# Local queries of a sparse attention spread into a block-diagonal tile of their own by GpSimd copies

## The chip, the cores and the metric

One core of a Trainium2 chip runs the whole program. The metric is the device time of one execution in microseconds (us). Engines are named as the profile names them: PE is TensorE (PEld its weight loads), DVE is VectorE, ACT is ScalarE, POOL is GpSimd, SP is SyncE, whose queue issues most of the DMA transfers.

## What is computed

An attention over 8 batches of 8 heads, 576 positions and 64 channels per head, all in fp32, followed by a mixture of 8 experts with one expert per token:

```
rel = pos[:, None] - pos[None, :]
mask_local = (rel >= 0) & (rel < 32)                      # heads 0 to 3
mask_strided = (rel >= 0) & (pos[None, :] % 32 == pos[:, None] % 32)   # heads 4 to 7
scores = where(mask, q @ k.T / 8, -1e9); attn = softmax(scores) @ v
x = attn as [4608 tokens, 512]; expert = argmax(x @ w_gate)
out[token] = gate[token] * (relu(x[token] @ w1[expert]) @ w2[expert])
```

Only the local heads are concerned here: each block of 32 queries needs the 64 keys of its own block and the one before it.

## The kernel before, in words

The attention is cut into 40 tasks, five for each batch (`tasks`, line 762). Tasks 0 and 1 of a batch (k = 0 and 1) each hold 16 query blocks of one pair of local heads; tasks 2 to 4 hold the rest of the local blocks and the strided heads. So task numbers 0, 1, 5, 6, 10, 11 and so on to 36 are the 16 local ones. Each task goes through four stages:

- `stage_s` (line 388): a matmul against the identity writes the mask into a PSUM bank (line 391), then small matmuls add the scores. In a local task they are 16 calls of `wide` (line 396), one for each query block: the stationary operand (the weights, 128 partitions by 64 columns) is block diagonal, the 32 queries of head h in partitions 64h to 64h+63 and zeros elsewhere, and the moving operand is the block's 64 keys of both heads. An fp32 matmul is two instruction pairs of load and matmul in the records, so a local task shows 32 of each on line 399, 512 in all.
- `softmax` (line 337): DVE takes maxima (`nm`, line 340) and subtracts, ACT takes the exponential, DVE sums and inverts (`ri`, line 349), POOL multiplies (line 350).
- `stage_t` (line 438), three tasks later (`LAG_T`): PE transposes the probabilities (line 441), ACT copies them out of PSUM.
- `av_local` and `av_strided`, four tasks later (`LAG_AV`): PE multiplies by the values (line 466 for the local heads, line 455 for the others).

The order of PE's instructions is that of the loop on line 790, by hand: in iteration i the transposes of task i-3, then the scores of task i, then the values of the batch that is complete. The order on the other engines is worked out by a scheduler, and each engine takes its own queue strictly in that order. After the scores of task i the loop calls `load_qk(i + 5)` (line 364), the queries and keys of the same k in the next batch, and `load_v`. Between the tasks of a batch PE also makes the routing to experts and, from the fourth batch on, the first expert tokens (`fillers`, line 632); their weight chunks of 1 MB come by `wload` (line 202) and are split into a high and a low part by `wsplit` (line 209: ACT casts on line 212, DVE subtracts on line 213). After the attention come the experts, on which the change has no hand.

The two local tasks of a batch have a tile each, `qkl[k]` (line 355), used again in every batch: 512 columns for head 0's queries, 512 for head 1's, 544 for the keys. The halves that must be zero are cleared once. `load_qk` fills the rest by three transfers of 64 partitions each. Queries lie there with the block number as the fast index, so that `wide` takes each 16th column:

```
q = qkl[k][:, 0:2 * LQ].rearrange("p (q j) -> p q j", j=LB)
k0 = 2 * LQ + QB * j
nc.tensor.matmul(sb[64 * i:64 * i + 64, col:col + 64], q[:, :, j], qkl[k][:, k0:k0 + 64],
                 start=False, stop=last, tile_position=(0, 64 * i))
```

With LB = 16 and 4 bytes an element, neighbouring columns of these weights are 64 bytes apart in a partition. The weights on line 466 (`vt[:, 64 * h:64 * h + 64]`) have the same shape and array position and lie in adjacent columns.

Of the kernel before, what the change touches and what calls it, by code (L numbers as in the profile page):

```python
# [7 lines left out]
F32 = mybir.dt.float32  # L8
# [9 lines left out]
B, S, D = 8, 576, 64  # L18
# [4 lines left out]
QB = 32  # L23
# [19 lines left out]
LAG_AV = 4  # L43
EXP = (0, 2, 4, 6)
# [92 lines left out]
def moe_attn(ctx, tc, qk, vv, wg, wcat, blob0, blob, out):  # L137
# [170 lines left out]
    with ExitStack() as actx:  # L308
        inp = actx.enter_context(tc.tile_pool(name="inp", bufs=NBK - 2))
# [45 lines left out]
        qkl = [loc.tile([128, 2 * LQ + LK], F32, name=f"qkl{k}") for k in range(2)]  # L355
        pTl = [loc.tile([128, 2, 512], F32, name=f"pTl{k}") for k in range(2)]
        for k in range(2):
            nc.vector.memset(qkl[k][64:128, 0:LQ], 0.0)
            nc.gpsimd.memset(qkl[k][0:64, LQ:2 * LQ], 0.0)
# [4 lines left out]
        def load_qk(i):  # L364
            if i < len(tasks):
                b, k = tasks[i]
                if k < 2:
                    o = QKO[k]
                    nc.sync.dma_start(out=qkl[k][64:128, LQ:], in_=qk[b, 64:128, o:o + LQ + LK])
                    nc.sync.dma_start(out=qkl[k][0:64, 0:LQ], in_=qk[b, 0:64, o:o + LQ])  # L370
                    nc.sync.dma_start(out=qkl[k][0:64, 2 * LQ:], in_=qk[b, 0:64, o + LQ:o + LQ + LK])
                    return
                t = inp.tile([128, max(QKW[2:])], F32, name="qk")
                loaded[b, "qk", k] = t
                nc.sync.dma_start(out=t[:, 0:QKW[k]], in_=qk[b, :, QKO[k]:QKO[k + 1]])

        def load_v(i):
            if i < len(tasks):
                b, k = tasks[i]
                t = inv.tile([128, VVW[0]], F32, name="vl", bufs=2) if k < 2 else inv.tile([128, max(VVW[2:])], F32, name="vt", bufs=3)  # L380
# [7 lines left out]
        def stage_s(b, k):  # L388
# [7 lines left out]
            def wide(j, i, col, last):  # L396
                q = qkl[k][:, 0:2 * LQ].rearrange("p (q j) -> p q j", j=LB)
                k0 = 2 * LQ + QB * j
                nc.tensor.matmul(sb[64 * i:64 * i + 64, col:col + 64], q[:, :, j], qkl[k][:, k0:k0 + 64],  # L399
# [254 lines left out]
        def slot_tables():  # L654
            rem = rt.tile([128, E], F32, name="rem")
            nc.vector.tensor_scalar(out=rem, in0=cnt, scalar1=-float(BASE), scalar2=0.0, op0=ALU.add, op1=ALU.max)
            it128 = rt.tile([128, 32], F32, name="it128")
# [118 lines left out]
        load_qk(0)  # L776
        nc.vector.tensor_copy(out=identb, in_=ident)
        make_masks()
        load_qk(1)
        load_qk(2)  # L780
# [8 lines left out]
        with tc.manual_schedule(engines={mybir.EngineType.PE}):  # L789
            for i in range(nt + LAG_AV):  # L790
# [14 lines left out]
                if i < nt:  # L805
                    filling()
                    pvs[i] = stage_s(*tasks[i])
                    load_qk(i + NBK)
# [170 lines left out]
def host_layout(q, k, v, moe_w_gate, moe_w1, moe_w2):  # L979
# [31 lines left out]
    for k in range(NBK):  # L1011
        for key, o in QK[k][0].items():
            o += QKO[k]
            if key == "l":
                parts = [lq[:, k, :, 0:LQ], lk[:, k, :, 0:LK]]
                parts[0] = parts[0].reshape(B, 128, LB, QB).transpose(0, 1, 3, 2).reshape(B, 128, LQ)
# [54 lines left out]
```

## Time and profile before

| what | us |
|---|---|
| median of 3 runs (lowest, highest) | 695.56 (695.17, 698.36) |
| the profiled execution, whole | 701.65 |
| its span, first to last instruction | 699.8 |
| outside the span (701.65 - 699.8) | 1.85 |
| PE busy in the span | 656.6 (94%) |
| DVE busy | 432.8 (62%) |
| ACT busy | 354.1 (51%) |
| POOL busy | 150.1 (21%) |

The profiled execution is one execution and was 6.09 us longer than the median of the runs. Its mean granted TensorE clock was 0.972. A busy PE is not PE at its peak: matmuls are pipelined and their ends are modelled, so the times from start to start in the timeline say more on its pace than the length of one. The attention takes roughly the first 215 us of the span; the first 95 us or so are attention alone.

### The profile page before, as it was taken

To read this page: it belongs to the slowest core of one execution; us is meant where nothing else is said; L and a number is where in the kernel's file an instruction comes from. 1 tells how busy PE (TensorE), PEld (TensorE's weight loads), DVE (VectorE), ACT (ScalarE), POOL (GpSimd) and SP (SyncE) were. 2 spreads that over 40 slices of the span, in tenths; PEclk is the share of its full clock that TensorE was granted. 3 is DMA by queue.
4 is the path that set the end of the run, shared out by engine and by line. 5 is a ranking of instruction groups with operands and counts; after the bars stand their busy time and mean duration, and the time that the engine had idled before them with its cause. 6 is when DMAs were issued, how large, how long until landed. Compare 5 with 4: busy or idle time off the path is not lost.

```text
span 699.8 us, 14771 instructions
## 1 busy us (share of the span) xinstructions
PE 656.6 (94%) x5996; PEld 548.9 (78%) x5996; DVE 432.8 (62%) x796; ACT 354.1 (51%) x617; POOL 150.1 (21%) x168
## 2 busy tenths in 40 slices
PE   5899799699989899999999999998999999999997
PEld 3777578587778778888888888887988878988885
DVE  5756768747476369888425867336675357583464
ACT  1556466455445455366225656336564246572363
POOL 3223222520311031127004132013132032010021
PEclk9999799999959999999999999999999999999999
DMA  9888989884842765558525968336766347765140
GB/s 284 257 239 251 303 255 294 287 290 141 286 129 92 287 215 174 193 208 304 234 112 166 352 215 286 117 133 234 296 245 223 120 138 270 267 225 180 61 180 21
DMA packets 36695, 149.85 MB, mean 214 GB/s; under 512 B 5261, under 2 KB 5645, under 8 KB 26384
## 3 DMA queue, kind: packets, MB, share of 16 engines
q1 hardware_dynamic: 24576, 118.50, 50.3%
q0 software_dynamic: 6432, 20.26, 8.1%
q10 hardware_dynamic: 5616, 10.12, 4.0%
q8 instruction: 48, 0.79, 0.5%
q14 instruction: 23, 0.19, 0.1%
HBM read 129.69 MB, written 20.22 MB: 214 GB/s over the span
## 4 chain that ended last, share of the span: by engine, by line
PE 72%; issue 13%; DVE 6%; ACT 4%; POOL 1%; another core or an unknown queue 1%; DMA 1%; POOLq 1%; SPq 0%; ACTq 0%
PE t L287 8%; PE t L288 7%; PE t L289 7%; PE y L276 6%; PE y L278 6%; PE y L277 6%; PE s L399 4%; PE t L441 2%; PE s L412 2%; PE v L265 2%; PE s L276 2%; PE s L278 2%; PE s L277 2%; PE v L455 1%; PE s L898 1%
## 5 line engine op out<-in xcount | busy, mean ns | idle before, releaser
L213 DVE TENSOR_TENSOR wlo<-raw,whi 128x1024 fp32r<-128x1024 f32 x160 | 192.6, 1221 | 88.4 <-ACT whi L212 76.6
L212 ACT CAST whi<-raw 128x1024 fp32r<-128x1024 f32 x160 | 163.3, 1050 | 67.5 <-PE s L278 26.1
L287 PE MATMUL t<-xh,whi 128*128 128x256 f32 (+1 forms) x384 | 126.1, 330 | 3.2 <-ACT xh L221 1.3
L288 PE MATMUL t<-xl,whi 128*128 128x256 f32 (+1 forms) x384 | 124.5, 325 | 0.3 <-DVE xl L222 0.3
L289 PE MATMUL t<-xh,wlo 128*128 128x256 f32 (+1 forms) x384 | 124.2, 324 | 0.0
L292 ACT ACTIVATE hh<-t 128x256 fp32r<-128x256 f32 (+1 forms) x96 | 43.5, 453 | 118.9 <-PE t L289 113.3
L293 DVE SCALAR_TENSOR_TENSOR hl<-t,hh 128x256 fp32r<-128x256 f32 (+1 forms) x96 | 48.9, 509 | 77.1 <-ACT hh L292 76.9
L287 PEld LDWEIGHTS t<-xh,whi 128*128 128x128 f32 x384 | 73.0, 191 | 11.7 <-ACT xh L221 2.1
L288 PEld LDWEIGHTS t<-xl,whi 128*128 128x128 f32 x384 | 73.4, 191 | 7.5 <-DVE xl L222 1.1
L289 PEld LDWEIGHTS t<-xh,wlo 128*128 128x128 f32 x384 | 73.2, 191 | 6.4 <-DVE wlo L213 0.8
L276 PE MATMUL y<-whi,hh 128*128 128x512 f32 x192 | 76.4, 398 | 0.0
L277 PE MATMUL y<-wlo,hh 128*128 128x512 f32 x192 | 75.1, 391 | 0.0
L278 PE MATMUL y<-whi,hl 128*128 128x512 f32 x192 | 75.0, 396 | 0.0
L350 POOL TENSOR_TENSOR prob<-prob,ri 128x512 f32<-128x512 f32 x40 | 43.4, 1084 | 147.2 <-DVE ri L349 91.8
L248 POOL DMA_INDIRECT out_dram<-y,oids x24 | 26.9, 1119 | 215.6 <-DVE y L247 166.6
L340 DVE TENSOR_REDUCE nm<-s 128x8 f32<-128x512 f32 x40 | 27.4, 686 | 29.7 <-PE s L399 19.5
L155 ACT COPY xT<-v 128x270 f32<-128x270 f32 (+1 forms) x80 | 30.2, 476 | 30.1 <-PE v L466 11.8
L278 PEld LDWEIGHTS y<-whi,hl 128*128 128x128 f32 x192 | 35.8, 188 | 8.4
L276 PEld LDWEIGHTS y<-whi,hh 128*128 128x128 f32 x192 | 36.2, 188 | 6.6 <-issue 0.8
L277 PEld LDWEIGHTS y<-wlo,hh 128*128 128x128 f32 x192 | 36.3, 189 | 5.7
L344 ACT ACTIVATE prob<-prob 128x512 f32<-128x512 f32 x40 | 25.3, 632 | 26.1 <-DVE prob L343 25.2
L399 PEld LDWEIGHTS s<-qkl 128*64 128x64 f32 x512 | 30.8, 209 | 8.1 <-issue 7.8
(173 smaller groups left out, 1170.9 us busy)
## 6 DMA issues: line engine op xcount, KB each, us to landing
raw<-in_wcat_dram SPq DMA_DIRECT2D x80, 1024.0 KB, 5.6
xd<-xr ACTq DMA_DIRECT2D x36, 264.0 KB, 5.5
vl<-in_vv_dram SPq DMA_DIRECT2D x16, 512.0 KB, 6.3
qkl<-in_qk_dram SPq DMA_DIRECT2D x16, 264.0 KB, 4.0
vt<-in_vv_dram SPq DMA_DIRECT2D x16, 256.0 KB, 5.6
qk<-in_qk_dram SPq DMA_DIRECT2D x8, 484.0 KB, 6.0
qk<-in_qk_dram SPq DMA_DIRECT2D x8, 432.0 KB
qk<-in_qk_dram SPq DMA_DIRECT2D x8, 396.0 KB, 5.7
```

The costliest lines, as they stand in the source:

```text
L212: nc.scalar.copy(out=hi[:, sl], in_=raw[:, sl])
L213: i = nc.vector.tensor_tensor(out=lo[:, sl], in0=raw[:, sl], in1=hi[:, sl].bitcast(F32), op=ALU.subtract)
L276: nc.tensor.matmul(yb[t], hh[:, ts], whi[:, w], start=(j == 0), stop=False)
L277: nc.tensor.matmul(yb[t], hh[:, ts], wlo[:, w], start=False, stop=False)
L278: nc.tensor.matmul(yb[t], hl[:, ts], whi[:, w], start=False, stop=(j == 7))
L287: nc.tensor.matmul(hb[:, 0:n], whi[:, w], xh[:, dc, :], start=(dc == 0), stop=False)
L288: nc.tensor.matmul(hb[:, 0:n], whi[:, w], xl[:, dc, :], start=False, stop=False)
L289: nc.tensor.matmul(hb[:, 0:n], wlo[:, w], xh[:, dc, :], start=False, stop=(dc == 3))
L292: nc.scalar.activation(out=hh[:, 0:n], in_=hb[:, 0:n], func=AF.Relu)
L293: nc.vector.scalar_tensor_tensor(out=hl[:, 0:n], in0=hb[:, 0:n], scalar=0.0, in1=hh[:, 0:n].bitcast(F32), op0=ALU.max, op1=ALU.subtract)
L350: lastp[0] = nc.gpsimd.tensor_tensor(out=pv, in0=pv, in1=ri.unsqueeze(2).broadcast_to([128, 8, 64]), op=ALU.mult)
L399: nc.tensor.matmul(sb[64 * i:64 * i + 64, col:col + 64], q[:, :, j], qkl[k][:, k0:k0 + 64], start=False, stop=last, tile_position=(0, 64 * i))
```

## The change

The queries get a tile of their own, `qbd[k]`, 16 blocks of 64 adjacent columns, zeroed once by DVE. `qkl[k]` holds 512 columns of queries and 544 of keys, as they come, for both heads one above the other, and is filled by one transfer of 128 partitions. `spread(i)` copies each head's queries from it to their place on the diagonal with two POOL copies of 64 partitions by 16 by 32 elements; it is called two tasks ahead (`AHEAD`). The loaded tiles of tasks 2 to 4 get a name and a buffer each instead of three buffers under one name, and one small table is put into a buffer that is in use anyway.

```diff
-        inp = actx.enter_context(tc.tile_pool(name="inp", bufs=NBK - 2))
+        inp = actx.enter_context(tc.tile_pool(name="inp", bufs=1))
...
-        qkl = [loc.tile([128, 2 * LQ + LK], F32, name=f"qkl{k}") for k in range(2)]
+        qkl = [loc.tile([128, LQ + LK], F32, name=f"qkl{k}") for k in range(2)]
+        qbd = [loc.tile([128, LB, 2 * QB], F32, name=f"qbd{k}") for k in range(2)]
...
-            nc.vector.memset(qkl[k][64:128, 0:LQ], 0.0)
-            nc.gpsimd.memset(qkl[k][0:64, LQ:2 * LQ], 0.0)
+            nc.vector.memset(qbd[k].rearrange("p j q -> p (j q)"), 0.0)
...
-                    o = QKO[k]
-                    nc.sync.dma_start(out=qkl[k][64:128, LQ:], in_=qk[b, 64:128, o:o + LQ + LK])
-                    nc.sync.dma_start(out=qkl[k][0:64, 0:LQ], in_=qk[b, 0:64, o:o + LQ])
-                    nc.sync.dma_start(out=qkl[k][0:64, 2 * LQ:], in_=qk[b, 0:64, o + LQ:o + LQ + LK])
+                    nc.sync.dma_start(out=qkl[k], in_=qk[b, :, QKO[k]:QKO[k + 1]])
                     return
-                t = inp.tile([128, max(QKW[2:])], F32, name="qk")
+                t = inp.tile([128, QKW[k]], F32, name=f"qk{k}")
...
+        def spread(i):
+            if i < len(tasks) and tasks[i][1] < 2:
+                k = tasks[i][1]
+                for h in range(2):
+                    hs = slice(64 * h, 64 * h + 64)
+                    nc.gpsimd.tensor_copy(out=qbd[k][hs, :, QB * h:QB * h + QB],
+                                          in_=qkl[k][hs, 0:LQ].rearrange("p (j q) -> p j q", q=QB))
...
-                q = qkl[k][:, 0:2 * LQ].rearrange("p (q j) -> p q j", j=LB)
-                k0 = 2 * LQ + QB * j
-                nc.tensor.matmul(sb[64 * i:64 * i + 64, col:col + 64], q[:, :, j], qkl[k][:, k0:k0 + 64],
+                k0 = LQ + QB * j
+                nc.tensor.matmul(sb[64 * i:64 * i + 64, col:col + 64], qbd[k][:, j, :], qkl[k][:, k0:k0 + 64],
                                  start=False, stop=last, tile_position=(0, 64 * i))
...
-            it128 = rt.tile([128, 32], F32, name="it128")
+            it128 = scratch(32)
...
                     pvs[i] = stage_s(*tasks[i])
+                    spread(i + AHEAD)
                     load_qk(i + NBK)
```

PE's own order is the same. On POOL the copies stand between the multiplications of the softmax, one of which belongs to each task (`prob` is a task's probabilities; the numbers behind the names are those of the buffers in the program). The multiplications of tasks 5 to 8 and the first rows of tokens (`xr`) in POOL's queue before:

```order
L350 TENSOR_TENSOR prob_389<-prob_389,ri_394 128x512
L350 TENSOR_TENSOR prob_466<-prob_466,ri_471 128x512
L350 TENSOR_TENSOR prob_511<-prob_511,ri_516 128x512
L350 TENSOR_TENSOR prob_585<-prob_585,ri_590 128x512
L505 COPY xr_688<-gt_328 128x16
```

and the same place now, from task 4's multiplication to that of task 8 (`qbd0` and `qkl0` belong to k = 0, here task 10, `qbd1` and `qkl1` to k = 1, here task 11):

```order
L351 TENSOR_TENSOR prob_347<-prob_347,ri_352 128x512
L380 COPY qbd0_135<-qkl0_133 64x16x32 x2
L351 TENSOR_TENSOR prob_389<-prob_389,ri_394 128x512
L351 TENSOR_TENSOR prob_464<-prob_464,ri_469 128x512
L380 COPY qbd1_136<-qkl1_134 64x16x32 x2
L351 TENSOR_TENSOR prob_507<-prob_507,ri_512 128x512
L351 TENSOR_TENSOR prob_581<-prob_581,ri_586 128x512
```

So the copies for task 10 stand ahead of the multiplication of task 5, and those for task 11 ahead of task 7's. A batch later the copies for tasks 15 and 16 stand between the multiplications of tasks 10 and 11:

```order
L351 TENSOR_TENSOR prob_673<-prob_673,ri_678 128x512
L351 TENSOR_TENSOR prob_742<-prob_742,ri_747 128x512
L380 COPY qbd0_135<-qkl0_133 64x16x32 x2
L380 COPY qbd1_136<-qkl1_134 64x16x32 x2
L351 TENSOR_TENSOR prob_817<-prob_817,ri_822 128x512
```

In the batches behind, the copies for task 20 stand ahead of task 15's multiplication, those for 21 ahead of 16's, those for 25 and 26 ahead of 21's, those for 30 ahead of 25's and those for 31 ahead of 26's.

On SP the weight chunks (`raw`) moved forward as well. Before, the first one was issued in the middle of the loads of the fifth batch (`vt` and `vl` are values):

```order
L375 DMA qk<-in_qk_dram 128x968
L382 DMA vt<-in_vv_dram 128x640
L375 DMA qk<-in_qk_dram 128x792
L382 DMA vt<-in_vv_dram 128x512 x2
L375 DMA qk<-in_qk_dram 128x864
L204 DMA raw<-in_wcat_dram 128x2048
L369 DMA qkl_133<-in_qk_dram 64x1056
L370 DMA qkl_133<-in_qk_dram 64x512
```

and now two stand among the loads of the third batch:

```order
L369 DMA qkl_134<-in_qk_dram 128x1056
L373 DMA qk_516<-in_qk_dram 128x968
L388 DMA vt_552<-in_vv_dram 128x640
L373 DMA qk_592<-in_qk_dram 128x792
L388 DMA vt_686<-in_vv_dram 128x512
L388 DMA vt_624<-in_vv_dram 128x512
L205 DMA raw<-in_wcat_dram 128x2048
L373 DMA qk_684<-in_qk_dram 128x864
L205 DMA raw<-in_wcat_dram 128x2048
L369 DMA qkl_133<-in_qk_dram 128x1056
```

With them their two pairs of casts on ACT and subtractions on DVE moved to the tasks around number 10.

## Rows read from the trace of the kernel before

**Rows 1.** The page: the span, and busy time, share of the span and instructions of each engine.

```profile
span 699.8 us, 14771 instructions
PE 656.6 (94%) x5996; PEld 548.9 (78%) x5996; DVE 432.8 (62%) x796; ACT 354.1 (51%) x617; POOL 150.1 (21%) x168
```

**Rows 2.** The chain of work that ended last, over the whole span: shares of the span by engine, tile written and line.

```profile
by line: issue 12.9%; PE t L287 7.6%; PE t L288 7.5%; PE t L289 7.5%; PE y L276 5.9%; PE y L278 5.9%; PE y L277 5.7%; PE s L399 4.0%; PE t L441 2.2%; PE s L412 1.8%; PE v L265 1.7%; PE s L276 1.6%; PE s L278 1.6%; PE s L277 1.6%; PE v L455 
```

**Rows 3.** Groups of instructions by line and shape over the whole span: line, engine, operation, tiles, weights as partitions*columns, out<-in, count | busy us, mean ns of one | idle us before them and what ended it.

```profile
L399 PE MATMUL s<-qkl 128*64 128x64 f32 x512 | 33.1, 289 | 2.0 <-DMA qkl<-in_qk_dram 2.0
L399 PEld LDWEIGHTS s<-qkl 128*64 128x64 f32 x512 | 30.8, 209 | 8.1 <-issue 7.8 <-DMA vl<-in_vv_dram 0.3
...
L412 PEld LDWEIGHTS s<-qk 64*54 64x54 f32 x640 | 21.2, 141 | 6.2 <-issue 3.6 <-DMA vt<-in_vv_dram 0.8 <-DMA qk<-in_qk_dram 0.5
...
L466 PE MATMUL v<-pTl,vl 128*64 128x64 f32 x512 | 17.3, 223 | 1.1 <-issue 1.0
...
L466 PEld LDWEIGHTS v<-pTl,vl 128*64 128x64 f32 x512 | 16.1, 138 | 1.7 <-issue 1.6
```

**Rows 4.** The same chain between 20 and 62 us: the shares of this stretch by line, then three of its pieces in order of time (start us, us, what).

```profile
by line: PE s L399 19.2%; ACT xT L155 11.4%; PE t L441 10.6%; PE v L455 9.3%; PE v L466 8.9%; PE s L412 7.7%; PE y L516 5.9%; ACT prob L344 4.7%; PE s L391 4.6%; PE y L508 4.6%; issue 3.7%; PE y L523 3.6%; POOL prob L350 2.5%; PE s L407 1.7
...
42.45 2.00 PE s L399 x32
44.45 1.87 PE v L466 x64
...
59.52 0.94 PE s L412 x32
```

**Rows 5.** Busy time of each engine in stretches of 20 us: stretch, its length, busy us (instructions) of PE, PEld, DVE, ACT and POOL, granted PE clock, busy share of the DMA engines, GB/s.

```profile
40.00:60.00 20.00, 19.68 (x395) 14.68 (x391) 13.12 (x34) 11.98 (x26) 5.75 (x9) 1.00 0.88 258
...
100.00:120.00 20.00, 19.00 (x330) 14.53 (x326) 15.86 (x47) 12.14 (x28) 6.11 (x11) 1.00 0.91 294
120.00:140.00 20.00, 14.28 (x323) 11.18 (x319) 16.36 (x43) 10.34 (x22) 9.87 (x8) 0.91 0.89 295
```

**Rows 6.** The timeline of PE in the first 20 us: start us, us, what, count [idle before <-releaser].

```profile
6.76 2.11 PE L399 MATMUL s<-qkl 128*64 128x64 f32 x32 [2.05 <-DMA qkl<-in_qk_dram]
8.79 0.61 PE L391 MATMUL s<-mask_b,identb 128*128 128x512 bf16 x1
...
16.89 1.63 PE L412 MATMUL s<-qk 64*54 64x54 f32 x32
```

**Rows 7.** The timeline of PE, the scores of tasks 5, 11, 16 and 26 (line 399), each followed by the transposes of the same task (line 441), and the routing matmul on line 606.

```profile
22.14 2.05 PE L399 MATMUL s<-qkl 128*64 128x64 f32 x32
...
31.51 0.66 PE L441 MATMUL t<-cst,prob 128*128 128x128 f32 x4
...
47.05 2.12 PE L399 MATMUL s<-qkl 128*64 128x64 f32 x32
...
57.39 0.66 PE L441 MATMUL t<-cst,prob 128*128 128x128 f32 x4
...
68.49 2.00 PE L399 MATMUL s<-qkl 128*64 128x64 f32 x32
...
77.62 0.66 PE L441 MATMUL t<-cst,prob 128*128 128x128 f32 x4 [0.66 <-POOL prob L350]
80.66 0.64 PE L606 MATMUL y<-bb,am 128*128 128x64 bf16 x9 [2.39 <-DVE bb L599]
...
115.96 2.06 PE L399 MATMUL s<-qkl 128*64 128x64 f32 x32
...
125.15 0.66 PE L441 MATMUL t<-cst,prob 128*128 128x128 f32 x4 [0.66 <-POOL prob L350]
```

**Rows 8.** POOL: two groups by shape (columns as in Rows 3), then the multiplications of tasks 5 and 16 in its timeline (columns as in Rows 6).

```profile
L350 POOL TENSOR_TENSOR prob<-prob,ri 128x512 f32<-128x512 f32 x40 | 43.4, 1084 | 147.2 <-DVE ri L349 91.8 <-DVE gt L538 13.1 <-PE s L412 8.3
...
L362 POOL MEMSET pTl<- 64x512 f32 x2 | 1.1, 530 | 0.1
...
27.80 1.04 POOL L350 TENSOR_TENSOR prob<-prob,ri 128x512 f32<-128x512 f32 x1 [2.23 <-DVE ri L349]
...
75.91 1.65 POOL L350 TENSOR_TENSOR prob<-prob,ri 128x512 f32<-128x512 f32 x1 [7.28 <-ACT prob L344]
```

**Rows 9.** DMA issues by line (out<-in, queue, count, KB each, median us from issue to landing), and for the tile qkl alone the times to landing.

```profile
vl<-in_vv_dram SPq DMA_DIRECT2D x16, 512.0 KB, 6.3
qkl<-in_qk_dram SPq DMA_DIRECT2D x16, 264.0 KB, 4.0
...
DMA to landing us min/median/max: 3.4/5.9/9.1
```

**Rows 10.** Who waited for whom between 0 and 200 us: us in total, times, longest us.

```profile
PE t L441 <- POOL prob L350: 4.8, 4, 2.4
...
DVE nm L340 <- PE s L399: 19.5, 12, 3.1
```

**Rows 11.** The subtraction that splits a weight chunk (group by shape), and the first issue of a chunk in SP's timeline.

```profile
L213 DVE TENSOR_TENSOR wlo<-raw,whi 128x1024 fp32r<-128x1024 f32 x160 | 192.6, 1221 | 88.4 <-ACT whi L212 76.6 <-issue 6.8 <-PE v L265 3.2
...
83.81 0.42 SPq L204 DMA_DIRECT2D raw<-in_wcat_dram  x1
```

More of the change, by code (lines that the diff above doesn't have):

```diff
@@ L43 @@
 LAG_AV = 4
+AHEAD = 2
 EXP = (0, 2, 4, 6)
@@ L379, in load_v @@
                 b, k = tasks[i]
-                t = inv.tile([128, VVW[0]], F32, name="vl", bufs=2) if k < 2 else inv.tile([128, max(VVW[2:])], F32, name="vt", bufs=3)
+                t = inv.tile([128, VVW[0]], F32, name="vl", bufs=2) if k < 2 else inv.tile([128, VVW[k]], F32, name=f"vt{k}", bufs=1)
                 loaded[b, "v", k] = t
@@ L776, in moe_attn @@
         load_qk(0)
+        spread(0)
         nc.vector.tensor_copy(out=identb, in_=ident)
@@ L779, in moe_attn @@
         load_qk(1)
+        spread(1)
         load_qk(2)
@@ L1015, in host_layout @@
                 parts = [lq[:, k, :, 0:LQ], lk[:, k, :, 0:LK]]
-                parts[0] = parts[0].reshape(B, 128, LB, QB).transpose(0, 1, 3, 2).reshape(B, 128, LQ)
             elif key[0] == "lx":
```

## The prediction

> **What bounds the kernel now.** I began with the page: in a span of 699.8 us PE is busy 94%, the next engine, DVE, 62%, POOL 21% [rows 1]. That PE is busy does not say that its work is the path, so next came the chain of waits. There the 512 score matmuls of the local tasks, line 399, hold 4.0% of the span, and no line outside the experts holds more [rows 2]. 4.0% of 699.8 is 28.0 us. Between 20 and 62 us, where the attention runs alone, the same line is the largest piece of the chain, 19.2% [rows 4]: these matmuls are on the path, not beside it.
>
> Then the groups by shape, to see whether they are slow for what they do. Line 466 multiplies with weights of the same 128 by 64, the same 64 moving columns and the same kind of array position. Its weight loads take 138 ns in the mean, those of line 399 209 ns, and those of line 412 with 54 adjacent columns 141 ns [rows 3]. These lengths overlap, so the pace is read from the chain: 32 passes of line 399 take 2.00 us, which is 62.5 ns each, 64 of line 466 take 1.87 us, 29.2 ns each, 32 of line 412 take 0.94 us, 29.4 ns each [rows 4]. What line 399 has and the others lack is that neighbouring columns of its weights are 64 bytes apart. I take that for the cause: its loads, not its multiplications, set the pace.
>
> **The change part by part.** *The weights become adjacent.* All 512 passes take 512 x 62.5 = 32.0 us; the chain holds 28.0 of them, or 87%. At full clock a pass falls from 62.5 to 29.2 ns, so a task of 32 saves 1.07 us. Tasks 0 and 1 run at the lower of PE's two clock levels: the mask matmul between them takes 0.61 us, and soon after 32 passes of 54 columns take 1.63 us, 51 ns each [rows 6]. Scaled to 64 columns that is 1.93 us for a task against 2.11 now, a saving of 0.2 each. So 14 x 1.07 + 2 x 0.2 = 15.4 us, and 87% of it, **13.4 us, lies on the path**.
>
> A rule of the Trainium skill speaks against this. The rows show that equal loads of adjacent columns pass every 29.2 ns [rows 4]. "TensorE: Matmul & The Clock Gate", section "LDWEIGHTS (loading the stationary operand)", has a load cost its columns divided by 1.2 in ns, wherever they lie: 64 columns would take some 53 ns before and after, and the 512 passes would give back about 5 us. The trace does not agree, since line 466 goes faster than that; the sum goes by its rows, and the rule is left to a rival.
>
> *POOL gets 32 copies* of 64 partitions by 512 elements. The trace shows none. From below, a memset of that shape takes 0.53 us; from above, the multiplication of 128 by 512 with two inputs takes 1.08 [rows 8]. I take 0.7, nearer to the operation with fewer inputs, and keep both ends. 22 us of work on an engine busy for 150 of 700 cost nothing by themselves. What can cost is the queue. The copies wait for the reload of `qkl`, whose transfer may start only when the matmuls that read the tile are done, and behind them in POOL's strict order waits a multiplication that PE's transposes need. From the end of a local task's scores, that multiplication is done after
>
> N = landing + two copies + one multiplication.
>
> For the landing of one whole transfer of 528 KB the trace has 3.4 us as the shortest for this tile, 4.0 as the median of the half-size part that goes first, 6.3 as the median of a 512 KB transfer, and 9.1 as the longest [rows 9]. I take 5.0: the reload is issued into a nearly empty queue, like the 4.0, with twice the bytes. So N = 5.0 + 1.4 + 1.1 = 7.5 us; the bounds are 3.4 + 1.1 + 1.1 = 5.6 and, with the median, 6.3 + 2.2 + 1.1 = 9.6.
>
> When is it due? Task 5's scores end at 22.14 + 2.05 = 24.19, its transposes start at 31.51, 7.3 later [rows 7]; between them task 6's scores become 1.1 shorter, so it is due at 6.2: **a stall of 1.3 us**. Task 11, behind the copies for tasks 15 and 16: 57.39 - 49.17 = 8.2, no stall. Tasks 16 and 26 would be ready for PE 0.66 before 77.62 and 125.15, which is 6.5 after their scores end: 1.0 of stall each. But PE waits there already, for this very multiplication, and at task 16 stands another 2.39 us at the routing matmul of line 606, which hangs on DVE [rows 7]; so I count nothing for these two. The other places leave 8.2 or more. At the upper bound the stalls would be 3.4 at task 5, 1.4 at task 11, some 0.7 each at tasks 16 and 26 beyond what DVE takes anyway, and 1 at three more places: about 9.
>
> *At the start* PE waits 2.05 us for the third of the three transfers and begins at 6.76 [rows 6]. One transfer instead of three is issued sooner by the two that fall away, and two copies of 0.7 come between landing and matmul. These are about even: 0, with 1 us on either side. DVE clears two tiles of 1,024 columns instead of two halves, during the same wait.
>
> *The weight chunks come earlier.* Before, the first chunk of 1 MB was issued at 83.81 us [rows 11]; now two are asked for in the third batch, near 40 us, and their four subtractions of 1.22 us [rows 11] go to DVE there. DVE is busy 13.12 of 20 us in that stretch [rows 5]; with 4.9 more it has 18.0, in a batch that takes some 20 us and is to take 18. I put this at 0: what DVE's queue holds up there is gone later, between 100 and 140 us, where it is busy 15.86 and 16.36 of 20 and PE waits for it.
>
> The sum: 13.4 - 1.3 = **12.1 us less**. The profiled execution took 701.65 us in all, so 689.6 for its like; it was 6 us above the median of the runs, 695.56, from which the same 12.1 leaves 683.5.
>
> **The rivals.** *DVE takes over* (16%). For: it is the next engine, its own wait for line 399 was 19.5 us in 12 places [rows 10], and with the subtractions the third batch would leave it no slack. Against: those waits say that DVE is behind PE now, not ahead. If half of the 13.4 us turns into waits for DVE: 6.7 - 1.3 = 5.4 less, 690.2.
>
> *A load costs by column, not by place* (6%), so that a pass stays near the 51 ns of [rows 6]: 512 x 11.5 ns = 5.9, 87% of it 5.1, less the stall 3.8: 691.8. Against it stands line 466. It is the rule of the Trainium skill that is weighed above.
>
> *More than the forecast* (9%): no stall, and all 15.4 us on the path: 680.2; reloads that come sooner in one piece could add 2.
>
> *Slower* (5%): POOL's strict order. If the reload lands like the longest, 9.1 us, and a copy costs 1.08, N = 12.4. Then task 5 stalls 6.2 us, task 11 4.2, tasks 16 and 26 together some 7 beyond DVE's wait, and tasks 15, 21 and 25, due 8.5 to 9 us after their scores, 3.6 each, 10.8: 28.2 in all, against 13.4 saved, so 14.8 more: 710.4. It decides from N of about 10.2 on, a landing of 7 us with dear copies. Against: PE waited for POOL only 4.8 us in 200 [rows 10], and the reloads that went out alone landed in about 4. One warning for it: beside a DVE instruction a multiplication took 1.65 instead of 1.04 [rows 8].
>
> **How the numbers follow.** The forecast holds 64%; its own bounds are 13.4 - 9 = 4.4 less (691) and 15.4 + 2 less (678). All of that is faster by over 0.5% (692.1), about what a measurement of this kernel can tell from no change; so are the better case, three quarters of DVE's case and half of the case by column: 64 + 9 + 12 + 3 = 88, of which I take off one for moves of the schedule that I didn't follow. Slower 5%, the rest, 8%, within 0.5%. The range of 677.5 to 691 leaves out the slow case, the case by column and the dear end of DVE's, together with little at the fast end.
>
> **What would show it.** Right: weight loads of the score matmuls at about 140 ns in the mean instead of 209, 32 passes in 0.95 us, and POOL copies of 0.6 to 0.8 us, with PE's waits for the multiplication up by a microsecond or two. Wrong: loads that stay near 200 ns; line 399's successor gone from the chain with DVE or ACT in its place and PE idle longer; or POOL waiting for the reload in each batch, and PE for POOL by more than 13 us.

## The result, and the profile after

The changed kernel takes 699.50 us in the median, the kernel before 695.39 in the same set of runs: ratio 1.0064, 95% interval 1.0041 to 1.0087. Two later sets gave 1.0035 (1.0010 to 1.0060) and 1.0025 (1.0000 to 1.0050). The forecast was 12.1 us less. A comparison leaves out executions more than 1.5% above the fastest of their kernel; here that is one, of e6. Runs e2, e11, e12, e15 and e17 rest on 6 executions each, e18 on 8, the others on 11 or 12.

The page of the changed kernel, to be read against [rows 1]:

```profile
span 695.6 us, 14757 instructions
PE 642.0 (92%) x5996; PEld 531.7 (76%) x5996; DVE 437.2 (63%) x796; ACT 354.7 (51%) x617; POOL 168.7 (24%) x198
```

PE is busy 14.6 us less than in [rows 1], as the faster passes should make it, yet the time is not lower. (This execution took 697.36 us, 2 under its median; that of [rows 1] was 6 over its own.) The groups that answer to [rows 3] and [rows 8], with line 399 now 404:

```profile
L380 POOL COPY qbd<-qkl 64x512 f32<-64x512 f32 x32 | 20.8, 650 | 27.1 <-DMA qkl<-in_qk_dram 17.8 <-PE v L460 4.9 <-PE t L446 3.3
L404 PE MATMUL s<-qkl,qbd 128*64 128x64 f32 x512 | 20.1, 237 | 0.0
L404 PEld LDWEIGHTS s<-qkl,qbd 128*64 128x64 f32 x512 | 17.8, 148 | 5.7 <-issue 4.4 <-POOL qbd L380 1.0 <-DMA qk<-in_qk_dram 0.3
```

Two lines of PE's timeline (columns as in [rows 6]), one after the other:

```profile
23.75 1.15 PE L404 MATMUL s<-qkl,qbd 128*64 128x64 f32 x32
24.73 2.04 PE L471 MATMUL v<-pTl,vl 128*64 128x64 f32 x64
```

32 passes now take 0.98 us from start to start, against 2.00 in [rows 4]; loads 148 ns against 209; a copy 0.65 us. The end of the first row is new: POOL stood 17.8 us waiting for reloads.

Where the saving went needs traces at a like clock. The first trace of before was of a long execution, so both kernels were traced again (runs e9 and e5 below, of two sets with nearly the same median for the kernel before; granted clock 0.972 and 0.975, spans 688.4 and 687.8). Up to the same instruction of PE near the end of the attention (the last value matmuls end 3.7 us later, at 237.1 and 234.3, not near 215 as said ahead), in the columns of [rows 5], first before, then changed:

```profile
0.00:233.40 233.40, 208.33 (x3409) 169.37 (x3410) 153.10 (x388) 124.58 (x251) 62.33 (x90) 0.92 0.77 248
```

```profile
0.00:230.60 230.60, 193.65 (x3409) 153.98 (x3410) 157.17 (x388) 125.30 (x251) 81.27 (x120) 0.93 0.73 250
```

PE's work fell by 14.7 us and its idle time rose from 25.1 to 37.0, by 11.9. So 2.8 us are left there. What PE waited for in these stretches, before:

```profile
PE y L606 <- DVE bb L599: 4.8, 2, 2.4
PE s L391 <- DVE mask_b L325: 4.2, 1, 4.2
PE t L441 <- POOL prob L350: 3.9, 3, 2.5
PE s L399 <- DMA qkl<-in_qk_dram: 1.9, 1, 1.9
...
PE v L455 <- issue: 0.3, 1, 0.3
```

and changed:

```profile
PE t L446 <- POOL prob L351: 9.1, 6, 4.0
PE s L397 <- DVE mask_b L326: 7.0, 1, 7.0
PE v L460 <- issue: 4.1, 2, 3.0
PE y L611 <- DVE bb L604: 2.2, 2, 1.5
...
PE s L417 <- issue: 2.0, 2, 1.3
```

Multiplications on POOL cost 5.2 more, "issue" (PE waits for nothing that the profile shows) 5.8 more, the start 0.9 more, DVE's `bb` 2.6 less; ACT and other waits of DVE make up the rest, some 2.6. Of the 9.1 us for multiplications, 4.0 stand at the transposes of task 0 (2.6 of 3.9 before), where no reload is waited for; the rest is at tasks 16, 21 and 26 (1.0, 1.4 and 2.3), with 0.4 at two earlier places together. The POOL wait answers to [rows 10]; in the first trace it rose from 4.8 to 8.7 in the first 200 us.

**The reloads.** The scores of task 11 on PE, and POOL's timeline around the copies for tasks 15 and 16 and the multiplications of tasks 11 and 12 behind them, second trace:

```profile
46.38 1.15 PE L404 MATMUL s<-qkl,qbd 128*64 128x64 f32 x32
```

```profile
52.10 2.23 POOL L380 COPY qbd<-qkl 64x512 f32<-64x512 f32 x2 [2.52 <-DMA qkl<-in_qk_dram]
55.33 2.12 POOL L380 COPY qbd<-qkl 64x512 f32<-64x512 f32 x2 [1.00 <-DMA qkl<-in_qk_dram]
57.53 2.04 POOL L351 TENSOR_TENSOR prob<-prob,ri 128x512 f32<-128x512 f32 x2
```

the second weight chunk's issue on SP, and the transfers issued between 40 and 50 us, with the median time to landing last:

```profile
40.98 0.42 SPq L205 DMA_DIRECT2D raw<-in_wcat_dram  x1
```

```profile
qkl<-in_qk_dram SPq DMA_DIRECT2D x2, 528.0 KB, 7.9
raw<-in_wcat_dram SPq DMA_DIRECT2D x1, 1024.0 KB, 9.0
vl<-in_vv_dram SPq DMA_DIRECT2D x2, 512.0 KB, 8.8
```

The reload lands in 7.9 us (8.1 and 7.6) beside a weight chunk and the values, not in 5.0. Each pair of copies then takes over 2 us, 1.1 for a copy, while DVE subtracts.

**The stops of PE.** In the same stretch PE stops in the middle of some 48 equal matmuls, and the packets of the stretch 52 to 56 us hold one of queue q8 (queue: packets, MB, share of 16 engines):

```profile
52.66 0.39 PE L460 MATMUL v<-pT,vt 54*64 54x54 f32 x11
56.02 1.18 PE L460 MATMUL v<-pT,vt 54*64 54x54 f32 x34 [2.97 <-issue]
```

```profile
q1 hardware_dynamic: 469, 1.60, 98.8%
q10 hardware_dynamic: 22, 0.04, 2.4%
q8 instruction: 1, 0.02, 1.4%
```

No wait for a semaphore ends there. The q8 packet ends at 54.63, and PE goes on 1.4 us later, while the data queues keep the DMA engines full. This trace has four such stops (near 35, 50, 56 and 79 us), 6.1 us of idle time in all, each ending 1.4 to 1.6 us after a q8 packet ends; the other two traces of the changed kernel have the same four (5.5 and 6.1 us), the two traces of before one each, near 35 us, of 0.7 and 0.3. The DMA engines are full between 48 and 58 us in both kernels, but move more in the changed one (columns as in [rows 5], second traces, first before):

```profile
48.00:58.00 10.00, 9.69 (x220) 6.14 (x218) 7.22 (x17) 6.13 (x15) 3.13 (x3) 1.00 1.02 287
```

```profile
48.00:58.00 10.00, 6.32 (x189) 4.82 (x187) 9.00 (x16) 7.74 (x15) 5.76 (x6) 0.90 0.97 389
```

Over an execution q8 carries 0.79 MB in 48 packets, and PE has 11,992 records (5,996 each on PE and PEld): 66 bytes for each. I read q8 as PE's own instructions, late behind the transfers. That is inferred and not shown: e1 and e14 below, with the weight chunks later, lose most of the stops, but so does e6, which keeps a chunk there. The Trainium skill, "Runtime: NRT & Kernel Launch", section "Instruction fetch mechanics", has instructions come in blocks of 16 KiB by a DMA queue of the sequencer, and the crossing of a block "mostly hidden". The packet size agrees (0.79 MB / 48). Most packets cost PE nothing in the changed kernel either, 11 of the 15 that end before 120 us; the other four go with the 6.1 us, a term that the forecast does not have.

**The clock.** The changed kernel between 55 and 58 us, second trace:

```profile
55.00:56.00 1.00, 0.00 (x0) 0.00 (x0) 1.00 (x3) 0.24 (x1) 0.67 (x1) 1.00 1.02 402
56.00:57.00 1.00, 0.98 (x34) 0.98 (x35) 1.00 (x3) 0.00 (x0) 0.96 (x2) 0.50 1.00 401
57.00:58.00 1.00, 1.00 (x15) 0.42 (x9) 0.00 (x0) 0.80 (x3) 0.92 (x2) 0.50 0.46 177
```

After the stop, 2.97 us in which PE did nothing, the granted clock is at the lower level (0.50, 1.2 GHz) until 59.4. Each of the three traces of the changed kernel has this low stretch; in [rows 5] and the second trace of before the clock is 1.00 from 40 to 60. Over whole traces no such difference shows: 34.9, 34.5 and 42.8 us at the lower level in the three of the changed kernel, 39.5 and 39.1 in the two of before. Over all executions of the set of e5 the mean granted clock was 0.973 against 0.981 before, in that of e13 0.969 against 0.975, and within a kernel an execution with 0.01 less took 4 us more (slopes 3.9 over 12 executions changed, 4.0 over 34 before; 2.8 and 3.4 in the set of e13). By the slope of 4, 0.008 is 3.2 us, an estimate; that the stops are what lowers the mean is not shown.

**After the attention** the changed kernel waits for tokens that POOL's gathers bring (205 to 285 us, second trace):

```profile
PE v L266 <- DMA xg<-xd,ids: 1.5, 2, 1.0
```

Before has no such wait; on POOL a gather and a scatter of rows now alternate where two gathers stood together. From that point of the attention to the seventh scatter of rows (near 300 us) the changed kernel lost 3.8 us on before in the first traces and 1.8 in the second.

The sum by the second traces: 14.7 saved, 11.9 idle, 1.8 after the attention, and 3.2 for the clock of a usual execution: 2.2 us slower. Measured in the set of e5, 0.35% of 688.64: 2.4 (0.7 to 4.1). That it comes so near is in part luck: the two traces were 0.003 apart in clock themselves, the other way, and with that the clock term is 4.4 and the sum 3.4 slower.

### The profile page after: what moved, and what is told of

It is laid out like the page before. It is cut to its first block, busy times and chain, and to the rows that moved or that the text cites. A ratio compares the mean times of both kernels' runs of the same rounds, so it can differ in the third digit from the quotient of the medians.

```text
span 695.6 us, 14757 instructions
## 1 busy us (share of the span) xinstructions
PE 642.0 (92%) x5996; PEld 531.7 (76%) x5996; DVE 437.2 (63%) x796; ACT 354.7 (51%) x617; POOL 168.7 (24%) x198
## 4 chain that ended last, share of the span: by engine, by line
PE 58%; issue 12%; DVE 5%; DMA 2%; ACT 2%; POOL 1%; POOLq 1%; ACTq 0%; another core or an unknown queue 0%
PE t L288 7%; PE t L289 7%; PE t L290 7%; PE y L277 6%; PE y L279 5%; PE y L278 5%; DVE wlo L214 2%; PE v L266 2%; PE s L277 2%; PE s L279 2%; PE s L278 2%; PE s L906 1%; PE s L907 1%; PE s L908 1%; PE v L513 1%
## 5 line engine op out<-in xcount | busy, mean ns | idle before, releaser
L288 PEld LDWEIGHTS t<-xh,whi 128*128 128x128 f32 x384 | 72.3, 189 | 11.6 <-issue 2.2
L351 POOL TENSOR_TENSOR prob<-prob,ri 128x512 f32<-128x512 f32 x40 | 41.6, 1046 | 92.9 <-DVE ri L350 55.4
L230 POOL DMA_INDIRECT xg<-xd,ids x24 | 30.5, 1270 | 32.5 <-DVE prob L677 19.5
```

The lines of the kernel that those rows point to most:

```text
L230: lastp[0] = nc.gpsimd.indirect_dma_start(out=xg, out_offset=None, in_=xd[0:rows, :], in_offset=bass.IndirectOffsetOnAxis(ap=idc, axis=0))
L288: nc.tensor.matmul(hb[:, 0:n], whi[:, w], xh[:, dc, :], start=(dc == 0), stop=False)
L351: lastp[0] = nc.gpsimd.tensor_tensor(out=pv, in0=pv, in1=ri.unsqueeze(2).broadcast_to([128, 8, 64]), op=ALU.mult)
```

## The experiments

Five sets, each on one chip with its own runs of the kernel before: e1 to e4 (before took 702.64 us there), e5 to e8 (688.64), e9 to e12 (688.16), e13 to e16 (701.54), e17 and e18 (688.44). Ratios are to these. Since one kernel differs by 2% between sets, two of them on the same chip (e5's and e13's), a difference within a set counts for more than one across sets. "Stops" are PE's idle time as above: put down to issue, in the middle of equal matmuls, ending 1.2 to 2.0 us after a q8 packet.

**e1_chunks_back, e14_chunks_back_again.** The first reload of batch 5 is remembered, and the chunks' transfers are ordered behind it:

```diff
+        i = nc.sync.dma_start(out=raw, in_=wcat[(e * NCH + c) * 128:(e * NCH + c + 1) * 128, :])
+        if lastq:
+            issue_after(i, lastq[0])
...
+                    if b == 5:
+                        lastq[:] = [i]
```

> The changed kernel with the first weight chunks held back behind the reload of batch 5's local queries and keys, so that the first four are asked for near 100 us and later, as in the kernel before, and not at 36 to 68 us; nothing else is edited. Theory A (the chunks that the scheduler moved forward crowd the queues: reloads land late, ACT and DVE have casts and subtractions in batches 2 to 4): the reloads of tasks 10 to 20 land in under 5 us, POOL's wait for them falls from 17.8 us to under 9, and the kernel takes 690 to 694 us, ratio to the kernel before 0.992 to 0.998. Theory B (POOL's strict order: copies that wait for the reload hold up the multiplications of the softmax, whoever else is on the queues): POOL still waits over 14 us for reloads, 697 to 700 us, ratio 1.002 to 1.007.

> The changed kernel with the first weight chunks held back behind batch 5, as once before. If the early chunks are a part of the loss (value tiles and reloads land late behind them: PE's wait at the value matmuls fell from 3.7 to 1.5 us with this edit), it is 3 to 6 us under the changed kernel of this set. If its 0.997 was the chip, it is within 2 us of it, and the waits only change their place.

Measured 0.9971 (0.9943 to 0.9999) and 0.9989 (0.9959 to 1.0019), the latter 2.7 us under the changed kernel of its set (1.0025), with overlapping intervals. The stops fell to 1.5 and 0.9 us, but PE's wait for multiplications rose from 9 to 11.7 and 11.6:

```profile
PE t L451 <- POOL prob L354: 11.7, 7, 4.0
...
PE v L465 <- issue: 1.5, 1, 1.5
```

POOL still waited 17.6 us for reloads in e1 and 14.6 in e14 (17.8 and 23.5 in the first two traces of the changed kernel), though the one reload of the third batch whose landing the traces tell took 6.0 and 6.2 us. So both theories hold a part, and half of what one gives back goes to the other's wait.

**e2_queries_early, e3_both.** Queries and keys in tiles of their own; the queries' transfer for task i+6 is asked for in iteration i:

```diff
+                    load_qk(i + NBK)
+                    load_q(i + NBK + 1)
```

> The changed kernel with queries and keys of the local tasks in two tiles and two transfers; the queries' transfer, whose tile only the copies read, is asked for an iteration after those copies, some five tasks before the next ones, so that no copy has to wait for a landing. Weight chunks stay early. Theory B (copies wait for the reload, multiplications wait behind them): POOL's wait for these transfers falls from 17.8 us to under 3, PE's wait for the multiplications from 8.7 to under 5, the multiplication of task 11 is back near 54 us from 57.9, and the kernel takes 687 to 692 us, ratio 0.988 to 0.995. Theory A (crowding by the weight chunks): the crowding stays, 696 to 700 us, ratio 1.001 to 1.007, with other waits in the same stretches, such as PE for the keys or for ACT.

> Both edits: queries in a transfer of their own, early, and the first weight chunks held back behind batch 5. If A and B are each a part of the loss, the saving of the passes comes out: 683 to 688 us, ratio 0.982 to 0.990. If one of them is all of it, this equals the better of the two kernels with one edit within 2 us. If the loss lies elsewhere (the start, 2 us, and waits of PE that are put down to issue), it stays above 695.

e2 gave 0.9843 (0.9796 to 0.9890) over 6 executions; e6, below, with this edit and one more, over 11 in another set, does not bear that out, so I do not lean on it. e3 gave 0.9981 (0.9953 to 1.0010): not the sum of two savings. POOL waits under 1 us for reloads in either; PE waits 5.1 and 4.9 us for multiplications. e3's idle time is still 38.2 us, with one wait of 5.7 us for ACT's `xT` that the changed kernel has not.

**e4_strided, e15_strided_again.** All of the change but the adjacency:

```diff
-        qbd = [loc.tile([128, LB, 2 * QB], F32, name=f"qbd{k}") for k in range(2)]
+        qbd = [loc.tile([128, 2 * QB, LB], F32, name=f"qbd{k}") for k in range(2)]
...
-qbd[k][:, j, :]
+qbd[k][:, :, j]
```

> The changed kernel, all of it, except that the block-diagonal tile keeps the block number as its fast index, so that neighbouring weight columns are 64 bytes apart again. It prices the adjacency alone under the new order. If the saving of the passes is real in the total and something else loses about 17 us: 32 passes take 2.0 us again and the kernel 711 to 714 us, ratio 1.022 to 1.027. Theory B (multiplications come too late for PE): each task leaves POOL 1.1 us more, so a good part of the saving was a wait in another place: 703 to 708 us, with PE's wait for POOL under 6 us in the first 200 in place of 8.7. If the adjacency gave nothing: 699 to 701.

> The changed kernel with weight columns 64 bytes apart, as once before. If the adjacency's saving comes out in the whole under the new order, as the traces to the end of the attention say (241 us against 231), this is 9 to 14 us above the changed kernel of this set, ratio to before 1.017 to 1.025. If most of it turns into waits, 3 to 6 us, ratio 1.007 to 1.012.

1.0080 (1.0047 to 1.0114) and 1.0157 (1.0124 to 1.0189), both under the 1.022 and 1.017 that the whole saving was to give at the least. The second stands beside the changed kernel on the same chip: 1.0157 - 1.0025 is 9.3 us that the adjacency brings (by the intervals 6 to 12). The first has no changed kernel in its set; against the 1.0025 to 1.0064 of the others it would be 1 to 4 us. Without the copies, e11 against e10 below, which differ in their chunks' times too, makes it 5.0 (2.6 to 7.3). So some 5 to 9 us of the saving do come out, and the rest of the change costs more than that. In e15, with the chunks as early as in the changed kernel (36.8 and 41.4 us), the stops are 2.0 (2.5 in e4): with slower passes come fewer of them.

**e5_after_again, e9_before_again, e13_after_third.** Both kernels unedited.

> The changed kernel itself, nothing edited, on the same chip as the three others of this set, since executions of one kernel differ here by some 8 us. Every theory: a ratio of 1.003 to 1.009 to the kernel before. If the late places of the first trace are the order of the work and not chance, the second trace has them again: the multiplication of task 11 over 3 us and that of task 16 over 4 us later than in the kernel before, and PE's wait for multiplications 7 us or more in the first 200.

> The kernel before, nothing edited, for a second trace of it: the first was of an execution 6 us over its median. Ratio 0.997 to 1.003. If the clock makes the difference between its executions, this trace has less time at the lower level in the first 240 us than the 38 us of the first, by about 2 us for each us that the execution is shorter, and the same idle time of PE up to the end of the attention, 28 us.

> The changed kernel, nothing edited, as the measure for the next two on the same chip. Ratio 1.002 to 1.008 to the kernel before, as on two chips so far.

1.0035, 0.9979 (0.9955 to 1.0004) and 1.0025. The late places came again: the transposes of task 16 5.8 us later than in the first trace of before in e5, 6.1 in e13, 5.7 in the first. Of e9's expectation the clock was wrong: its trace has as much at the lower level in the first 240 us as the first, 37.5 and 37.6 us, and 25.1 us of idle time, not 28.

**e6_early_and_masks, e12_no_copies_masks, e17_no_copies_masks_again, e18_adjacent_dma_masks.** One line, on top of e2, of e7 and of e11:

```diff
-        nc.scalar.dma_start(out=cst0, in_=blob0)
+        nc.sync.dma_start(out=cst0, in_=blob0)
```

> The kernel with the queries in an early transfer of their own, with one more edit: the transfer of the identity and the masks goes first in SP's queue, where the first large transfers stand, in place of ACT's queue beside them. Theory D (at the start the large transfers delay the masks, for which DVE and so PE's first matmul wait): the first mask matmul starts at 4.0 to 4.8 us in place of 5.87 (6.61 in the changed kernel, 4.12 before), all later tasks move up by a microsecond, and the kernel takes 0.982 to 0.989 of the time before. If the first score matmuls wait for the copies anyway, the start moves by less than 0.5 us and the ratio is that of the kernel without the edit.

> The kernel without copies (block diagonal with its zeros laid out in the input, 784 KB a transfer), and the masks' transfer first in SP's queue. Theory D: the first mask matmul moves from 6.97 us to 4.0 to 4.8, the first scores start when the first 784 KB are there, near 5.5, and the ratio falls from 0.991 to 0.986 to 0.990. If the large transfer sets the start anyway, 0.990 to 0.993.

> Block diagonal with its zeros from the input by one transfer, no copies, the masks' transfer first in SP's queue; nothing held back. As once before: ratio 0.985 to 0.991. If 0.993 to 0.997 comes out, it was the set, and holding the chunks back costs nothing; if 0.988 stands, holding them back took away 0.7%.

> Adjacent columns filled by transfers in pieces of 128 bytes, as before at 0.993, and the masks' transfer first in SP's queue. There PE's first matmul waited for the masks to 4.2 us and the first scores then 3.7 us more for the tile. If the tile sets the start, the masks first delay it by their own landing: 0.993 to 0.996. If the two come one after the other sooner, 0.989 to 0.992.

At the start of the changed kernel DVE waits for the masks, and PE for DVE; in e12 less so:

```profile
5.30 0.63 DVE L783 CAST identb<-cst 128x128 bf16<-128x128 f32 x1 [2.09 <-DMA cst<-in_blob_dram]
...
6.61 0.58 PE L397 MATMUL s<-mask_b,identb 128*128 128x512 bf16 x1 [6.61 <-DVE mask_b L326]
```

```profile
4.22 0.59 PE L392 MATMUL s<-mask_b,identb 128*128 128x512 bf16 x1 [4.22 <-DVE mask_b L326]
6.33 1.97 PE L399 MATMUL s<-qkl 128*64 128x64 f32 x32 [1.53 <-DMA qkl<-in_qk_dram]
```

Before, the masks had landed by 3.21 us. e6 gave 0.9981 (0.9950 to 1.0012), short of the 0.982 to 0.989 expected: early queries and masks together are worth 0.5% of the changed kernel's 1.0035. Its first mask matmul starts at 4.30 us, a chunk is issued at 37.9 and its stops are 1.1 us. e12 gave 0.9879 (0.9853 to 0.9905) and e17 0.9893 (0.9868 to 0.9919), e18 0.9915 (0.9892 to 0.9939): on e7 and e11 the edit is worth 0.2 to 0.3% and 0.1%, with overlapping intervals.

**e7_no_copies, e16_no_copies_masks_chunks.** The block diagonal with its zeros lies in the input array; one transfer of 784 KB, no copies (e16 with the masks first and the chunks held back):

```diff
-        qkl = [loc.tile([128, LQ + LK], F32, name=f"qkl{k}") for k in range(2)]
-        qbd = [loc.tile([128, LB, 2 * QB], F32, name=f"qbd{k}") for k in range(2)]
+        qkl = [loc.tile([128, 2 * LQ + LK], F32, name=f"qkl{k}") for k in range(2)]
+        qbd = [t[:, 0:2 * LQ].rearrange("p (j q) -> p j q", q=2 * QB) for t in qkl]
```

> The block diagonal, zeros included, is laid out in the input array, adjacent columns, and comes with the keys by one transfer of 784 KB; there are no POOL copies and no second tile. So the adjacency stands without anything new on POOL, at 256 KB more for each of 16 transfers. Theory B (copies that wait for the reload, in POOL's strict order): the reloads have five tasks of time, PE's wait for multiplications falls to under 5 us in the first 200 and the kernel takes 0.982 to 0.990 of the time before. Theory A (crowded transfers): it is no better than the changed kernel, 1.003 or more. Theory D: the start is later than the changed kernel's by 1 to 2 us, since 784 KB come ahead of the masks.

> Block diagonal with its zeros from the input by one transfer, no copies, the masks' transfer first, and the weight chunks held back behind batch 5. The kernel without the last edit took 0.988 of the time before and had 4.2 us of waits of PE that no record explains, at matmuls of the values and scores, where large transfers stand ahead of theirs. If those are the chunks, they go and the ratio is 0.980 to 0.985; if not, 0.986 to 0.990.

e7: 0.9912 (0.9882 to 0.9941), 8.5 us under the changed kernel of its set, 7.0 in the medians. Up to the end of the attention:

```profile
0.00:223.60 223.60, 192.96 (x3409) 152.71 (x3410) 151.80 (x386) 124.57 (x251) 61.36 (x88) 0.93 0.77 277
```

PE's work is that of the changed kernel, its idle time 30.6 and not 37.0. PE waits 4.0 us for multiplications, as before, the stops are 3.6, and there is no wait for gathers after the attention. But the scheduler moved the weight chunks with this edit too. The first is issued in e7 at:

```profile
61.31 0.42 SPq L205 DMA_DIRECT2D raw<-in_wcat_dram  x1
```

The third batch's reloads of 784 KB land in 5.9 and 6.7 us with no chunk beside them. So e7 takes away the copies and the early chunks together. It shows that 256 KB more a transfer cost less than both, and does not decide between theories A and B. e16, 0.9951 (0.9928 to 0.9974), is no gain over e12 and e17, as far as sets can be compared; the chunks held back further, to 97.7 us, did not help (stops 3.9).

**e8_copies_twice.** `for h in (0, 1, 0, 1)` in `spread`.

> The changed kernel with every copy made twice, the same data to the same place, so that 32 more copies of 0.65 us stand in POOL's queue: 1.3 us more between the reload's landing and the multiplication behind it, at 14 places. Theory B: the places at which PE waits for a multiplication, some six, get up to 1.3 us longer each: 4 to 9 us more than the changed kernel, ratio 1.010 to 1.019. Theory A: POOL is idle three quarters of the time and nothing moves, 1.003 to 1.009.

1.0031 (1.0002 to 1.0060): no slower than the changed kernel's 1.0035. Yet PE's wait for multiplications moved as theory B has it, and at task 11, where the changed kernel had its stop, PE now waits for POOL:

```profile
PE t L446 <- POOL prob L351: 14.3, 8, 4.0
```

```profile
59.91 0.97 PE L446 MATMUL t<-cst,prob 128*128 128x128 f32 x4 [2.26 <-POOL prob L351]
```

5.2 us more than in e5, while the stops fell from 6.1 to 1.1. My reading is that a PE that is held up by POOL leaves its instructions the time to arrive, so that the two waits are in part the same time and neither sum of waits is the price of its cause. A rival stands beside it, for this edit moved the chunks as well, the first two to 21.61 and 36.61 us, and the reloads of the third batch land sooner:

```profile
21.61 0.42 SPq L205 DMA_DIRECT2D raw<-in_wcat_dram  x1
...
36.61 0.42 SPq L205 DMA_DIRECT2D raw<-in_wcat_dram  x1
```

```profile
qkl<-in_qk_dram SPq DMA_DIRECT2D x2, 528.0 KB, 5.3
```

```profile
POOL qbd L380 <- DMA qkl<-in_qk_dram: 11.5, 5, 4.2
```

5.3 us and not 7.9, and POOL waits 11.5 us for reloads, not 23.5 as in e5. The mean granted clock of its executions was higher too, 0.978 against 0.973, some 2 us by the slope above. So what the doubled copies cost by themselves stays open.

**e10_step16, e11_adjacent_by_dma.** The kernel before, with the block number interleaved by 4 and by 1; two transfers of queries go straight into the diagonal:

```diff
-                q = qkl[k][:, 0:2 * LQ].rearrange("p (q j) -> p q j", j=LB)
+                q = qkl[k][:, 0:2 * LQ].rearrange("p (g q j) -> p g q j", q=2 * QB, j=STEP)
...
+                                          in_=qk[b, hs, o:o + LQ].rearrange("p (g x) -> p g x", x=STEP * QB))
```

> The kernel before, with the block number interleaved by 4 and not by 16, so that neighbouring weight columns are 16 bytes apart and not 64. The block diagonal is still filled by transfers alone, two of 64 partitions for the queries in pieces of 512 bytes and one for the keys; no copies, no second tile. If 16 bytes are near enough, 32 passes take 0.95 to 1.1 us, PE's idle time stays near 28 us since nothing new waits, and the kernel takes 0.982 to 0.990 of the time before: then the loss in the changed kernel is its copies and reloads. If every distance costs the same, 32 passes take 2.0 us and the ratio is 0.997 to 1.003. If the passes are fast and the ratio is still above 0.995, the saving cannot come out in this kernel at all, whatever fills the tile (PE waits for DVE and ACT, or a lower clock takes it).

> The same with the block number not interleaved at all: adjacent columns, filled by transfers in pieces of 128 bytes, 16 for each partition and head. 32 passes take 0.95 to 1.0 us. If the small pieces are dear, the transfers land after 9 us or more, the DMA engines' share rises, PE waits for tiles, and the ratio is over 1.0; if they cost no more than the 528 KB that they carry, 0.980 to 0.990. The scheduler asks for no weight chunk before 100 us here.

e10: 1.0000 (0.9981 to 1.0020). Its passes, and those of e11:

```profile
L404 PE MATMUL s<-qkl 128*64 128x64 f32 x512 | 34.2, 289 | 2.8 <-DMA qkl<-in_qk_dram 2.8
L404 PEld LDWEIGHTS s<-qkl 128*64 128x64 f32 x512 | 32.0, 215 | 8.8 <-issue 8.5 <-DMA raw<-in_wcat_dram 0.3
```

```profile
L404 PEld LDWEIGHTS s<-qkl 128*64 128x64 f32 x512 | 18.5, 153 | 9.9 <-issue 9.6 <-DMA qk<-in_qk_dram 0.3
```

and the landing of e11's queries in the first 200 us:

```profile
qkl<-in_qk_dram SPq DMA_DIRECT2D x32, 128.0 KB, 5.2
```

16 bytes apart costs what 64 did: 215 and 209 ns. Of the distances tried only adjacent columns are fast. e11 gave 0.9928 (0.9901 to 0.9956); pieces of 128 bytes land in 5.2 us. It has no copies, its first chunk goes out at 120.0 us (e10's at 60.8), and its stops are 1.0 us.

## Why the prediction was wrong, point by point

- *The passes*: right. 0.98 us for 32 where 0.95 was said, and 14.7 us of PE's work where 15.4 was. The rival by column is out: by the Trainium skill, "TensorE: Matmul & The Clock Gate", section "LDWEIGHTS (loading the stationary operand)", a load's time goes by its columns alone, for 64 of them an estimate of 53 ns; rows show 31 adjacent (0.98 / 32) and 62.5 apart.
- *87% on the path, 13.4 us*: too much. The adjacency brought 9.3 (6 to 12) by e15, 5.0 (2.6 to 7.3) by e10 and e11.
- *N = 7.5, landing 5.0*: the step that failed first. For task 5 it fits: N was 6.9 in the second trace, and PE waited 0.2 us there where 1.3 was said. In the third batch the landing was 7.6 to 8.1, and the two copies behind it took 2.1 us in that trace where 1.4 was said (0.65 for one is the mean). The scores of task 11 end at 47.53 and its multiplication at 58.58, so N was 11.0 (11.3 in the first trace), above the 9.6 of the upper bound and the 10.2 from which the rival with POOL's strict order decides. The reason for 5.0, a reload that is issued into a nearly empty queue, does not hold beside the prediction's own item on the weight chunks: one was issued at 40.98, the reloads at 43.85 and 47.61. That rival had 5%. Its N came, 11.0 at task 11 and 10.2 at task 16; its price did not. PE's wait rose by 5.2 us, not by 28, and 1.4 of that stands at task 0. At task 11 PE waited for nothing on POOL, since it had itself stopped for 2.97 us and came later.
- *The weight chunks at 0*: wrong in what was counted. I priced their subtractions on DVE, not their transfers. Beside these the reloads and values landed in 8 to 9 us. Held back, a reload lands in 6.0 to 6.2 us and the stops fall to 0.9 to 1.5; the gain, 2.7 us, is not separated from none by one set. Nor are the chunks all of it: e6 issues one at 37.9 us and has stops of 1.1.
- *The start at 0 (1 either side)*: 1.8 late at the first transposes. The copies were looked at, not the masks, for which DVE waited to 5.30 us instead of 3.21. That the whole transfers delay them is not shown by itself; in e12, with the masks first, PE begins at 4.22.
- *Nothing after the attention, and all at one clock*: 1.8 to 3.8 us at the gathers and, by the slope, some 3 us of clock were not in the sum.

What of the change costs the most: the copies with their reload and the early chunks, together. Without both, e7, 8.5 us come back (5.8 to 11.1), about what the adjacency brings. How these 8.5 divide between POOL's queue, the chunks, the stops and the gathers stays open: no run takes away the copies and leaves the chunks where they were.

The kernel that beats both, over 6 executions in each of two sets, is e12/e17: no copies, masks first, 0.9879 and 0.9893.

## What to carry to other kernels

Weights want adjacent columns; a step of 16 bytes was no better than one of 64. Fill such a layout where the data is laid out or by the transfer, not by copies in the queue of an engine whose other work is due. A transfer moved forward is to be priced on the DMA engines, by what else then lands late, perhaps the engines' own instructions among it. And an edit in one place can move transfers in another, as in e7 and e8: look at where each transfer is issued before a run is read as a test of one cause.

## What the runs showed of the hardware

- A strided load costs the same at 16 and at 64 bytes: 215 and 209 ns in the mean; adjacent 138 to 153.
- PE stopped in the middle of equal matmuls for 0.7 to 3.3 us, four times in each of three traces, each stop ending 1.3 to 1.7 us after a packet of queue q8 (kind "instruction"), the longest where the DMA engines were full (share 0.97). That PE had run out of instructions is inferred.
- Transfers of 128 KB in pieces of 128 bytes landed in 5.2 us in the median.
- The landing of a 528 KB reload: 7.6 and 8.1 us beside a chunk of 1 MB and the values, 4.9 and 5.7 in e8 with the chunks elsewhere.
- A copy of 64 by 512 elements on POOL took 0.65 us in the mean and 1.1 in the third batch of the second trace, while DVE was at work (2.23 and 2.12 for two).
